# Values of two batches by head on 96 partitions, their keys read in thirds with a stride, three weight loads moved

## The chip, the core and the metric

The kernel runs on one core of a Trainium2 chip, as a single program. Its time is in device microseconds (us). The engines of the core run side by side and wait for one another by semaphores: PE (TensorE: matmuls and transposes into PSUM), DVE (VectorE), ACT (ScalarE), POOL (GpSimd), and SP (SyncE), which here only issues transfers (DMAs). PSUM is the small memory that PE writes, SBUF the working memory of 128 partitions.

## What is computed

Eight batches of attention in two steps, and a layer of eight experts behind it. Everything is fp32.

```python
# q, k, v: 8 batches x 8 heads x 576 x 64; p: 8 x 8 x 32 x 64
p_packed = softmax(p @ k.T / 8) @ v          # 32 packed rows a head
out      = softmax(q @ p_packed.T / 8) @ p_packed
x  = out.transpose(0, 2, 1, 3).reshape(4608, 512)
logits = normed(x) @ normed(expert_emb).T / tau
e  = argmax(logits);  gate = softmax(logits)[e]
y  = gate * (relu(x @ w1[e]) @ w2[e])        # w1: 8 x 512 x 1024, w2: 8 x 1024 x 512
```

## The kernel before

The batches go through the core one after another. The kernel guesses one expert for a whole batch, loads its two weight matrices (w1, 2 MB, and w2, 2 MB), and runs the two matmul layers (`ffn`). While PE does the layers of a batch, the attention of the next one is slipped in between, by generators that are advanced one step at a time. The order on each engine is therefore fixed in the program. For batch 0 it is written out by hand, in the table `PLAN`, whose letters advance `begin` (q), the second softmax of batch 0 (s), the attention of batch 1 (a), the turning of batch 1's queries (d) and the splitting of w2 (w).

`begin` is the attention of batch 0 from an empty chip, and the scores of batch 1. Nothing can hide behind matmuls there; the work is a chain. PE warms up on constants (`WARM`, line 1252). Keys, values and queries of four heads (a group; g is 0 or 1) are loaded (`load_whole`, `load_v`). A loaded key tile, `nat`, has head and i on its 128 partitions, and in a row 18 keys of 64 numbers: key s = 18 i + c. PE turns it in nine blocks of 128 columns (`turn`, line 1264) into PSUM, and ACT or DVE copies the turned blocks into `kT` (tile `spare`). `parity_scores` (line 1296) multiplies the packed rows with the turned keys. It reads 288 of them as nine runs of 32 numbers that stand together. The runs are put in such an order (`blocks`) that the 96 keys of one chunk of weights are those of 32 partitions times three blocks, as `load_v` lays the values out: three transfers for each group, each to 32 partitions, four heads of 1,536 bytes in each partition. `p1_turn` turns the exponentials (line 473), and `pack_values` (line 486) multiplies them with the values.

PSUM tiles of the tag `pf` are three banks in rotation: a tile waits until the copy out of the third tile before it is done. The tile `pu` is one bank of its own, `pt` are two double banks.

Every transfer of SP and ACT waits for the landing of the one eight transfers before it. In the listings of the order this is `waits DMAHW0` to `DMAHW7`, eight semaphores in rotation. The transfers of SP are issued in program order, and one that waits holds up all behind it.

After the scores of batch 0's queries, `begin` issues in one go: the four loads of w2 (`load_w2`, line 960, 512 KB each, two of the eight blocks of w2 in each), the values of batch 1 (`load_v`), and its queries (`load_nat`, line 201, sixteen transfers of 140 KB). Then it turns batch 1's keys and makes its scores. Batch 1's queries are turned on DVE (`flip`, line 298, four of them, into `kt`). In DVE's order they stand between the copies behind PE's matmuls (lines 1072 and 1077) and the rows `ppx` of batch 1 (line 500), which PE then turns (line 510). PE needs all four for the scores of line 277. w2 is split on ACT and POOL (`split_w2`, lines 970 and 971), eight times for a batch, block by block; line 1102 also reads it as it was loaded.

Of the kernel before, what the change touches and what calls it, by code (L numbers as in the profile page):

```python
# [9 lines left out]
F32 = mybir.dt.float32  # L10
# [7 lines left out]
P = 128  # L18
HB = 4
NC5 = 5  # L20
KC = 6
KR = 96
# [5 lines left out]
def kernel(  # L28
# [12 lines left out]
    nc = tc.nc  # L41
# [185 lines left out]
    def load_v(b, g, odd=nc.sync):  # L227
# [36 lines left out]
    def head(g, c):  # L264

        return c ^ g
# [688 lines left out]
    def load_w2(x, e, queue=nc.sync):  # L955
        x.w2r = []
        w2e = w2[e].rearrange("(a p) m -> p a m", p=P)
        for i in range(NF // 2):
# [3 lines left out]
        x.w2s = []  # L962
# [259 lines left out]
    def begin():  # L1222
# [17 lines left out]
        vn = [load_v(0, g, nc.scalar) for g in range(NG)]  # L1240
# [3 lines left out]
        def bank():  # L1244
            return ps.tile([P, 512], F32, name="pf", tag="pf")
# [22 lines left out]
        def blocks(at, to):  # L1268
            return [m % 3 * 3 + m // 3 for m in range(at, to)]

# [19 lines left out]
        def parity_scores(to, w, t, g, at):  # L1290

            t = t[:, g].rearrange("p (c r i) -> p c r i", r=HB, i=32)
            for c in range(HB):
                for par in range(2):
# [4 lines left out]
                        t[hs, :, head(g, c)],  # L1299
# [6 lines left out]
        wx = scaled(pn, nc.vector)  # L1306
# [5 lines left out]
        def one_bank():  # L1312
            return pc.tile([P, 512], F32, name="pu", tag="pu")
# [12 lines left out]
        turn_keys(1, 0, 4, bank(), copies[0])  # L1326
        turn_keys(1, 4, 6, bank(), copies[1])
        pu = one_bank()
        turn_keys(1, 6, 9, pu, copies[0])
        kn1 = [load_whole(k[1], g) for g in range(NG)]  # L1330
        for g in range(NG):
            parity_scores(x.s1[g], wx, kT, g, lambda c: head(g, c))
# [75 lines left out]
        for g in range(NG):  # L1408
            parity_scores(s2[g], x.Tw, qT, g, lambda c: c)
# [21 lines left out]
        for g in range(NG):  # L1431
            turn(kn1[g], pu[:, g * P :], (8,))
        nc.scalar.copy(kT[:, :, 1024:], pu[:, : NG * P].rearrange("p (g s) -> p g s", g=NG))
        for n in range(2 * NG):
            if n:
                yield
            pu = bank()
            turn(kn1[n // 2], pu, blocks(n % 2 * 4, n % 2 * 4 + 4))
            nc.scalar.copy(kT[:, n // 2, n % 2 * 512 : n % 2 * 512 + 512], pu)
        yield  # L1440
        y.halves = True
        for g in range(NG):
            y.s1[g] = turn_bank()
            parity_scores(y.s1[g], wy, kT, g, lambda c: head(g, c))
            yield
# [50 lines left out]
    WARM = (4, 4)  # L1496
# [189 lines left out]
```

## Time and profile before

| | us |
|---|---|
| median of three runs | 412.43 |
| lowest, highest of them | 412.36, 414.54 |
| the profiled execution | 413.43 |
| its span, first to last instruction | 411.8 |
| PE busy | 402.9 |
| DVE, ACT, POOL busy | 310.1, 203.9, 161.2 |

The profiled execution took 413.43 us, of which 411.8 are its span and 1.6 lie around it; it was 1.0 us over the median. The granted TensorE clock is 0.999 of full speed over the span. PE is busy for 98% of the span, so the few microseconds in which it isn't, and those in which it waits inside a row, are what a change outside PE's own work can win.

### The profile page before, as it was taken

How to read it: one execution, taken by the hardware profiler on the slowest of the kernel's cores; microseconds unless marked ns; L12 is line 12 of the kernel's file. 1: busy time of each engine (PE TensorE's matmuls, PEld its weight loads, DVE VectorE, ACT ScalarE, POOL GpSimd, SP SyncE). 2: the span in 40 equal slices, each digit the busy share in tenths (PEclk: the TensorE clock that was granted, in tenths of full speed). 3: DMA queues.
4: the chain of work that ended last, by engine and by line, in shares of the span. 5: the costliest groups of instructions: out<-in, count | busy, mean ns of one | idle time of the engine just before them, and what ended most of it. 6: DMA issues, size and time to landing. Idle time of an engine off the chain costs nothing.

```text
span 411.8 us, 11101 instructions
## 1 busy us (share of the span) xinstructions
PE 402.9 (98%) x4012; PEld 322.4 (78%) x4013; DVE 310.1 (75%) x984; ACT 203.9 (50%) x507; POOL 161.2 (39%) x202
## 2 busy tenths in 40 slices
PE   7999999999999999999999999999999999999995
PEld 3758588697878978698786978789687987879785
DVE  3576888589996889779896899968897698836700
ACT  4677354763257622765138622667237651475201
POOL 2355802337503474047703375035730477030500
PEclk9999999999999999999999999999999999999999
DMA  8999898885889679985897768995799722910022
GB/s 226 337 335 211 217 275 297 223 202 163 249 327 238 163 191 345 286 206 139 215 394 213 206 169 265 332 234 146 203 333 281 200 66 77 391 39 19 8 61 56
DMA packets 42607, 87.93 MB, mean 214 GB/s; under 512 B 11690, under 2 KB 20906, under 8 KB 42546
## 3 DMA queue, kind: packets, MB, share of 16 engines
q1 hardware_dynamic: 35280, 61.44, 54.5%
q0 software_dynamic: 6720, 25.17, 16.7%
q10 hardware_dynamic: 546, 0.54, 0.6%
q8 instruction: 34, 0.56, 0.6%
q14 instruction: 27, 0.22, 0.2%
HBM read 77.68 MB, written 9.44 MB: 212 GB/s over the span
## 4 chain that ended last, share of the span: by engine, by line
PE 90%; DMA 6%; DVE 1%; SPq 0%; ACT 0%; issue 0%; DVEq 0%; ACTq 0%
PE pf L1120 43%; PE pf L1067 23%; PE pf L1102 7%; DMA vn<-in_v 4%; PE pt L995 3%; PE pt L797 3%; PE pt L277 2%; PE pt L403 2%; PE pt L338 2%; PE pu L797 2%; DMA nat<-in_k 1%; DMA nat<-in_q 1%; PE pf L1264 1%; PE pt L1296 0%; PE pu L510 0%; PE pf L486 0%
## 5 line engine op out<-in xcount | busy, mean ns | idle before, releaser
L1120 PE MATMUL pf<-w2s,hT 128*128 128x512 f32 (+1 forms) x792 | 181.5, 387 | 0.0
L1120 PEld LDWEIGHTS pf<-w2s,hT 128*128 128x128 f32 x792 | 143.7, 188 | 38.5 <-issue 10.1
L971 POOL TENSOR_TENSOR w2s<-w2r,w2s 128x512 fp32r<-128x512 f32 x64 | 80.8, 1287 | 73.3 <-ACT w2s L970 68.5
L1067 PE MATMUL pf<-AT,G 128*128 128x288 f32 x720 | 102.3, 299 | 0.3 <-DVE h L1077 0.3
L1067 PEld LDWEIGHTS pf<-AT,G 128*128 128x128 f32 x720 | 97.3, 188 | 4.0 <-issue 1.5
L1072 DVE SCALAR_TENSOR_TENSOR hT<-pf,hT 128x224 fp32r<-128x224 f32 (+1 forms) x128 | 52.3, 413 | 29.0 <-ACT hT L1071 28.6
L1071 ACT ACTIVATE hT<-pf 128x224 fp32r<-128x224 f32 (+1 forms) x128 | 49.3, 386 | 43.0 <-PE pf L1067 40.1
L298 DVE STREAM_TRANSPOSE kt<-nat 128x576 f32<-128x576 f32 x52 | 38.0, 757 | 2.5 <-DMA nat<-in_q 2.3
L1474 ACT ACTIVATE o<-pf,gate 128x512 f32<-128x512 f32 (+1 forms) x41 | 25.9, 634 | 24.4 <-PE pf L1120 16.8
L970 ACT CAST w2s<-w2r 128x512 fp32r<-128x512 f32 x64 | 37.7, 624 | 0.0
L891 POOL MEMSET oh<- 64x8 f32 x8 | 0.8, 98 | 86.2 <-DVE oh L887 86.2
L716 ACT ACTIVATE st<-st 128x576 f32<-128x576 f32 (+1 forms) x17 | 11.1, 658 | 43.8 <-DVE st L713 42.7
L1102 PE MATMUL pf<-w2r,h 128*64 128x256 f32 x256 | 31.5, 385 | 0.0
L1010 DVE TENSOR_TENSOR G<-pt,G 128x1024 fp32r<-128x1024 f32 x14 | 16.5, 1219 | 13.0 <-ACT G L1009 12.9
L933 ACT ACTIVATE lg<-lg 128x40 f32<-128x40 f32 x8 | 1.9, 237 | 48.3 <-DVE lg L929 48.3
L390 POOL TENSOR_TENSOR qs<-p 128x320 f32<-128x320 f32 x12 | 10.5, 877 | 36.9 <-ACT p L371 36.9
L1102 PEld LDWEIGHTS pf<-w2r,h 128*64 128x64 f32 x256 | 16.9, 137 | 8.5 <-PE pu L510 1.0
L810 ACT ACTIVATE scr<-pt 128x512 f32<-128x512 f32 (+1 forms) x32 | 15.7, 491 | 13.8 <-DVE part L851 10.6
L737 ACT CAST AT<-at 128x576 fp32r<-128x576 f32 x15 | 10.1, 675 | 17.9 <-DVE at L731 17.8
L371 ACT ACTIVATE p<-pt,qnm 128x160 f32<-128x160 f32 x48 | 17.8, 398 | 0.0
L960 POOL DMA_DIRECT2D w2r<-in_moe_w x24 | 16.9, 716 | 0.0
L702 DVE STREAM_TRANSPOSE st<-pt 128x288 f32<-128x288 f32 x32 | 13.3, 451 | 0.9 <-PE pt L1296 0.9
(235 smaller groups left out, 518.1 us busy)
## 6 DMA issues: line engine op xcount, KB each, us to landing
nat<-in_q SPq DMA_DIRECT2D x112, 140.0 KB, 3.4
nat<-in_k SPq DMA_DIRECT2D x96, 140.0 KB, 3.5
w1t<-in_moe_w POOLq DMA_DIRECT2D x12, 1024.0 KB, 7.6
w2r<-in_moe_w POOLq DMA_DIRECT2D x24, 512.0 KB, 9.7
out<-o SPq DMA_DIRECT2D x124, 64.0 KB, 2.6
w2r<-in_moe_w SPq DMA_DIRECT2D x8, 512.0 KB, 10.6
vn<-in_v SPq DMA_DIRECT2D x24, 160.0 KB, 3.7
vn<-in_v SPq DMA_DIRECT2D x48, 80.0 KB, 3.7
```

The source lines that it names most:

```text
L298: nc.vector.transpose(kt.rearrange("p (c i) -> p c i", i=32), t)
L371: nc.scalar.activation(x.p1[g][:, n * QW : n * QW + QW], area(x, g)[:, n // 2, n % 2], AF.Exp, bias=x.nm[:, at : at + 1],)
L797: nc.tensor.matmul(to, x.at[at, g, tokens], x.ppx[at, g], start=True, stop=True, tile_position=(64 * half, column),)
L960: queue.dma_start(t, w2e[:, 2 * i : 2 * i + 2, :])
L970: nc.scalar.copy(t[:, 0], raw)
L971: nc.gpsimd.tensor_tensor(out=t[:, 1], in0=raw, in1=t[:, 0].bitcast(F32), op=ALU.subtract)
L1067: nc.tensor.matmul(pf[:, :HS], w, r, start=(n == 0), stop=(n == len(ops) - 1))
L1071: nc.scalar.activation(hT[:, 0, f, cs], pf[:, :n], AF.Relu)
L1072: nc.vector.scalar_tensor_tensor(out=hT[:, 1, f, cs], in0=pf[:, :n], scalar=0.0, in1=hT[:, 0, f, cs].bitcast(F32), op0=ALU.max, op1=ALU.su ...
L1102: nc.tensor.matmul(pf[64 * hf : 64 * hf + 64, :256], h4[:, f], x.w2r[f // 2][:, f % 2, hf * 256 : hf * 256 + 256], start=(f == 0), stop=(f ...
L1120: nc.tensor.matmul(pf[:, :w], hT[:, a, f, c * P : (c + 1) * P], x.w2s[f][:, m, at : at + w], start=(f == 0 and i == 0), stop=(f == NF - 1 ...
L1474: nc.scalar.activation(o[:, :w], pf[:, :w], AF.Copy, scale=x.gate[:, c : c + 1])
```

## The change

There are four edits.

- `load_v` brings the values of a head in one transfer to 96 partitions: partition p holds keys 6 p to 6 p + 5, 1,536 bytes for each head. A group takes four transfers instead of three. All eight of batch 0 are SP's; before, two of its six were ACT's. Batches 2 to 7 load by `load_runs` and are as they were.
- A chunk of 96 keys is now every sixth key, so the scores must come out in that order. The nine blocks of a group are turned in thirds, as they lie, three to a bank (`turn_keys`), for batch 0 and batch 1 alike. `key_scores` reads the turned keys with the third as the innermost index: consecutive numbers of the moving operand stand 384 numbers (1,536 bytes) apart. The output is as wide as before. The scores of the queries (line 1296 with `tw`) read as before.
- The packed rows of batch 0 are turned ahead of the keys on PE, and the second of the two warm-up matmuls is 384 columns wide instead of 512.
- Three of the four loads of batch 0's w2 stand behind batch 1's values and queries on SP.

```diff
     def load_v(b, g):
         t = sb.tile([P, KC * HB * D], F32, name="vn", tag="vn", bufs=2)
         t = t.rearrange("p (h w) -> p h w", h=HB)
-        s = v[b, g * HB : (g + 1) * HB].rearrange("h (i c) d -> i h (c d)", c=NCB)
-        for a in (0, 2, 1):
-            (odd if a == 2 else nc.sync).dma_start(
-                t[32 * a : 32 * a + 32], s[:, :, a * KC * D : (a + 1) * KC * D]
-            )
+        s = v[b, g * HB : (g + 1) * HB].rearrange("h (p c) d -> h p (c d)", c=KC)
+        for h in range(HB):
+            nc.sync.dma_start(t[:KR, h], s[h])
...
-        def turn_keys(g, at, to, pu, copy):
-            pu = pu[:, : (to - at) * P]
-            turn(kn[g], pu, blocks(at, to))
-            copy(kT[:, g, at * P : to * P], pu)
+        def turn_keys(nat, g, a, pu, copy):
+            turn(nat, pu, range(3 * a, 3 * a + 3))
+            copy(kT[:, g, 3 * a * P : 3 * a * P + 3 * P], pu[:, : 3 * P])
+
+        def key_scores(x, w, g):
+            t = kT[:, g].rearrange("p (a c r i) -> p r c i a", a=3, c=3, r=HB)
+            parity_scores(x.s1[g], w, t, lambda c: head(g, c), g)
+
+        wx = packed_turn(scaled(pn, nc.vector), one_bank())
...
-        turn_keys(0, 0, 4, bank(), copies[0])
-        turn_keys(0, 4, 8, bank(), copies[1])
-        turn_keys(0, 8, 9, x.s1[0][:, 384:512], copies[1])
-        wx = packed_turn(wx, one_bank())
-        turn_keys(1, 0, 4, bank(), copies[0])
-        turn_keys(1, 4, 6, bank(), copies[1])
+        for n in range(5):
+            turn_keys(kn[n // 3], n // 3, n % 3, bank(), copies[n != 1 and n != 3])
         pu = one_bank()
-        turn_keys(1, 6, 9, pu, copies[0])
+        turn_keys(kn[1], 1, 2, pu, copies[0])
...
-        load_w2(x, x.e)
+        load_w2(x, x.e, pairs=range(1))
         for g in range(NG):
             loaded[1, 2 * NPR + g] = load_v(1, g)
         prefetch(order[1, NPR] + 3)
+        load_w2(x, x.e, pairs=range(1, NF // 2))
         yield
         wy = packed_turn(wy, bank())
-        pu = bank()
-        for g in range(NG):
-            turn(kn1[g], pu[:, g * P :], (8,))
-        nc.scalar.copy(kT[:, :, 1024:], pu[:, : NG * P].rearrange("p (g s) -> p g s", g=NG))
-        for n in range(2 * NG):
-            if n:
+        for n in range(3 * NG):
+            turn_keys(kn1[n // 3], n // 3, n % 3, bank(), nc.scalar.copy)
+            if n not in (0, 3):
                 yield
-            pu = bank()
-            turn(kn1[n // 2], pu, blocks(n % 2 * 4, n % 2 * 4 + 4))
-            nc.scalar.copy(kT[:, n // 2, n % 2 * 512 : n % 2 * 512 + 512], pu)
-        yield
...
-    WARM = (4, 4)
+    WARM = (4, 3)
```

SP's order from batch 0's second weights on. `w2r` are the four loads of w2, `vn` the values of batch 1, `nat<-in_q` its queries, `nat<-in_k` the keys of batch 2. Before:

```order
L960 DMA w2r<-in_moe_w 128x2x512
L960 ISA
L960 DMA w2r<-in_moe_w 128x2x512
L960 ISA
L960 DMA w2r<-in_moe_w 128x2x512
L960 ISA
L960 DMA w2r<-in_moe_w 128x2x512
L232 DMA vn<-in_v 32x4x384 x6
L201 DMA nat<-in_q 32x1120 x16
L201 DMA nat<-in_k 32x1120 x4
```

and changed:

```order
L959 DMA w2r<-in_moe_w 128x2x512
L232 DMA vn<-in_v 96x384 x8
L201 DMA nat<-in_q 32x1120 x16
L959 ISA
L959 DMA w2r<-in_moe_w 128x2x512
L959 ISA
L959 DMA w2r<-in_moe_w 128x2x512
L959 ISA
L959 DMA w2r<-in_moe_w 128x2x512
L201 DMA nat<-in_k 32x1120 x4
```

Twenty-four transfers instead of six and three weights stand between the first and the second load of w2.

ACT's order where batch 1's keys are turned. `wp` are the packed rows, `spare` the turned keys, `st` the exponentials of batch 0's second softmax (two, each behind POOL's subtraction), `g` rows of the first layer. Before:

```order
L1284 COPY wp<-pf 128x2x128
L1433 COPY spare<-pf 128x2x128
L1439 COPY spare<-pf 128x512
L716 ACTIVATE st<-st 128x288 x2
L1439 COPY spare<-pf 128x512 x3
L1047 COPY g_550<-pf 128x512 x2
```

and changed:

```order
L1279 COPY wp<-pf 128x2x128
L1305 COPY spare<-pf 128x384 x2
L714 ACTIVATE st<-st 128x288 x2
L1305 COPY spare<-pf 128x384 x4
L1045 COPY g_557<-pf 128x512 x2
```

Four copies instead of three stand behind the exponentials; with the three banks of `pf`, the matmul that fills `g` first waited for the first of these three, and waits for the second of these four.

## Rows read from the trace of the kernel before

**Rows 1.** The page: busy time, share of the span and instructions of each engine.

```profile
PE 402.9 (98%) x4012; PEld 322.4 (78%) x4013; DVE 310.1 (75%) x984; ACT 203.9 (50%) x507; POOL 161.2 (39%) x202
```

**Rows 2.** Chain of waits, 0 to 60 us: start, duration, what held the end.

```profile
1.46 5.33 DMA nat<-in_k
...
21.27 14.76 DMA vn<-in_v
...
36.85 4.73 DMA nat<-in_q
```

**Rows 3.** Timeline of PE at the start: start, duration, instruction, idle time before it.

```profile
1.23 3.78 PE L1252 MATMUL pf<-fill 128*128 128x512 f32 x4 [1.23 <-DVE mask L72]
5.21 1.06 PE L1264 MATMUL pf<-ident,nat 128*128 128x128 f32 x8 [0.20 <-DMA nat<-in_k]
...
17.22 0.72 PE L1296 MATMUL pt<-spare,tw 64*32 64x288 f32 x16
...
22.13 0.63 PE L1035 MATMUL pf<-w1t,tw 64*32 64x512 f32 x4 [0.54 <-ACT spare L1439]
```

**Rows 4.** Timeline of ACT at the start.

```profile
20.77 0.82 ACT L716 ACTIVATE st<-st 128x288 f32<-128x288 f32 x2
21.50 1.54 ACT L1439 COPY spare<-pf 128x512 f32<-128x512 f32 x3
```

**Rows 5.** Timeline of DVE, 39 to 49 us.

```profile
41.66 0.78 DVE L298 STREAM_TRANSPOSE kt<-nat 128x576 f32<-128x576 f32 x1 [1.58 <-DMA nat<-in_q]
...
44.95 0.59 DVE L500 SCALAR_TENSOR_TENSOR ppx<-pt,ri,mask 128x128 f32<-128x128 f32 x2
...
48.02 0.78 DVE L298 STREAM_TRANSPOSE kt<-nat 128x576 f32<-128x576 f32 x1 [0.68 <-DMA nat<-in_q]
```

**Rows 6.** Timeline of PE, 24 to 60 us.

```profile
28.57 5.12 PE L1067 MATMUL pf<-at,g 128*128 128x288 f32 x20
...
43.66 1.08 PE L1102 MATMUL pf<-w2r,h 128*64 128x256 f32 x8
45.34 0.59 PE L510 MATMUL pu<-ident,ppx 128*128 128x128 f32 x2 [0.59 <-DVE ppx L500]
...
48.27 1.75 PE L277 MATMUL pt<-kt,T 64*32 64x288 f32 x32
```

**Rows 7.** Chain of waits over the whole span, at lines 277 and 510.

```profile
48.34 1.68 PE pt L277 x32
...
96.50 0.22 PE pu L510 x2
...
100.55 1.13 PE pt L277 x32
```

**Rows 8.** Timeline of SP's transfers, 16 to 52 us.

```profile
18.86 2.32 SPq L960 DMA_DIRECT2D w2r<-in_moe_w  x4
...
32.85 11.19 SPq L201 DMA_DIRECT2D nat<-in_q  x16
```

**Rows 9.** Tile w2r, 16 to 55 us: issue to landing of its four loads.

```profile
DMA to landing us min/median/max: 9.6/11.6/14.5
```

**Rows 10.** Windows: length, engines' busy time, clock, DMA share, GB/s; weights, values, queries.

```profile
24.00:29.00 5.00, 4.99 (x41) 2.79 (x31) 2.97 (x9) 3.21 (x7) 1.88 (x3) 1.00 1.05 398
30.00:35.00 5.00, 5.00 (x28) 4.18 (x26) 3.90 (x9) 4.13 (x10) 4.12 (x4) 1.00 1.10 193
38.00:45.00 7.00, 6.75 (x136) 5.75 (x134) 5.23 (x21) 5.99 (x15) 3.29 (x3) 1.00 0.94 251
```

**Rows 11.** Timeline of ACT, 41 to 43.5 us.

```profile
41.78 0.62 ACT L970 CAST w2s<-w2r 128x512 fp32r<-128x512 f32 x1
42.29 0.36 ACT L1071 ACTIVATE hT<-pf 128x224 fp32r<-128x224 f32 x1
```

**Rows 12.** Lines 1447 and 707 alone: durations in ns, times, forms.

```profile
L1447 DVE TENSOR_REDUCE fold<-ident x1: 380/380/380, 34.9 to 34.9; 128x32 f32<-128x128 f32 x1
L707 DVE TENSOR_REDUCE mx<-st x17: 453/752/754, 19.0 to 349.4; 128x18 f32<-128x576 f32 x15, 128x9 f32<-128x288 f32 x2
```

More of the change, by code (lines that the diff above doesn't have):

```diff
@@ L953, in load_w1, with load_w2 @@
         x.w1t = w1t
-    def load_w2(x, e, queue=nc.sync):
-        x.w2r = []
+    def load_w2(x, e, queue=nc.sync, pairs=range(NF // 2)):
+        if 0 in pairs:
+            x.w2r, x.w2s = [], []
         w2e = w2[e].rearrange("(a p) m -> p a m", p=P)
-        for i in range(NF // 2):
+        for i in pairs:
             t = sb.tile([P, 2, DM], F32, name="w2r", tag="w2r", bufs=NF // 2)
@@ L961, in load_w2 @@
             x.w2r.append(t)
-        x.w2s = []
     def split_w2(x):
@@ L1239, in begin @@
         next(emb_gen)
-        vn = [load_v(0, g, nc.scalar) for g in range(NG)]
+        vn = [load_v(0, g) for g in range(NG)]
         qn = [load_whole(q[0], g) for g in range(NG)]
@@ L1266, in turn @@
                 )
-        def blocks(at, to):
-            return [m % 3 * 3 + m // 3 for m in range(at, to)]
         def scaled(t, eng):
@@ L1288, in packed_turn, with parity_scores @@
             return to
-        def parity_scores(to, w, t, g, at):
-            t = t[:, g].rearrange("p (c r i) -> p c r i", r=HB, i=32)
+        def parity_scores(to, w, t, at, g):
             for c in range(HB):
@@ L1298, in parity_scores @@
                         w[hs, g * P + 32 * at(c) : g * P + 32 * at(c) + 32],
-                        t[hs, :, head(g, c)],
+                        t[hs, head(g, c)],
                         start=True,
@@ L1305, in begin, with one_bank @@
         x.halves = True
-        wx = scaled(pn, nc.vector)
+        def one_bank():
+            return pc.tile([P, 512], F32, name="pu", tag="pu")
+        def turn_keys(nat, g, a, pu, copy):
[5 more added lines that the diff above has]
+        wx = packed_turn(scaled(pn, nc.vector), one_bank())
         next(emb_gen)
@@ L1310, in begin @@
         copies = (nc.scalar.copy, nc.vector.tensor_copy)
[L1312 to L1318 removed]
         for g in range(NG):
             x.s1[g] = turn_bank()
[L1322 to L1327 removed]
+        for n in range(5):
+            turn_keys(kn[n // 3], n // 3, n % 3, bank(), copies[n != 1 and n != 3])
         pu = one_bank()
[L1329 removed]
+        turn_keys(kn[1], 1, 2, pu, copies[0])
+        key_scores(x, wx, 0)
         kn1 = [load_whole(k[1], g) for g in range(NG)]
[L1331 to L1332 removed]
+        key_scores(x, wx, 1)
         nc.tensor.matmul(pu[:, 384:385], fill[:1], tau1, start=True, stop=True)
@@ L1408, in begin @@
         for g in range(NG):
-            parity_scores(s2[g], x.Tw, qT, g, lambda c: c)
+            t = qT[:, g].rearrange("p (c r i) -> p r c i", r=HB, i=32)
+            parity_scores(s2[g], x.Tw, t, lambda c: c, g)
         pts = [one_bank(), bank()]
@@ L1427, in begin @@
         prefetch(order[1, NPR] + 3)
+        load_w2(x, x.e, pairs=range(1, NF // 2))
         yield
         wy = packed_turn(wy, bank())
-        pu = bank()
-        for g in range(NG):
-            turn(kn1[g], pu[:, g * P :], (8,))
-        nc.scalar.copy(kT[:, :, 1024:], pu[:, : NG * P].rearrange("p (g s) -> p g s", g=NG))
-        for n in range(2 * NG):
-            if n:
+        for n in range(3 * NG):
+            turn_keys(kn1[n // 3], n // 3, n % 3, bank(), nc.scalar.copy)
+            if n not in (0, 3):
                 yield
-            pu = bank()
-            turn(kn1[n // 2], pu, blocks(n % 2 * 4, n % 2 * 4 + 4))
-            nc.scalar.copy(kT[:, n // 2, n % 2 * 512 : n % 2 * 512 + 512], pu)
-        yield
         y.halves = True
@@ L1443, in begin @@
             y.s1[g] = turn_bank()
-            parity_scores(y.s1[g], wy, kT, g, lambda c: head(g, c))
+            key_scores(y, wy, g)
             yield
```

2 lines of the change are left out of this document (1 added, 1 removed).

## The prediction

> **What bounds the kernel now.** I read four views, in this order. The page first: PE is busy for 402.9 of 411.8 us [rows 1], so outside PE some 9 us are to be had at most, and where PE doesn't wait nothing is. Then the chain of waits for the first 60 us: it begins on the landing of batch 0's keys (issued at 1.46, 5.33 us), runs over PE, DVE and ACT without slack, and at 21.27 it leaves PE for a transfer of batch 1's values that lands 14.76 us later; from there it goes to a transfer of batch 1's queries [rows 2]. Behind 54 us the chain is PE alone, in a pattern that repeats from batch to batch. So the change can only act before 54 us, and what it wins or loses there is carried to the end unaltered. Third, the timelines of PE, ACT and DVE in that stretch, for the idle time in front of each instruction: PE waits 0.54 us for a copy of turned keys [rows 3] and 0.59 us for `ppx` [rows 6], and DVE twice waits for queries, 1.58 and 0.68 us [rows 5]. Last, SP's transfers, for what stands in front of those queries: four loads of w2 from 18.86 on, then values, and the first query is issued at 32.85 only [rows 8].
>
> **The start, up to 19 us: 0.** The warm-up takes 3.78 us for two matmuls (four records) [rows 3]. [...] 128 of 1,024 columns less are 0.47 us less; the two transposes of packed rows take that place. Both lie in front of the keys, for which PE waited 0.20 us [rows 3], and that wait is the cover: if it went, the difference of the two, about 0.1 us, would show. Batch 0's values now come in eight transfers of SP alone. The last of them waits for the landing of the second keys, at 6.8 us [rows 2]; at the slowest rate of the trace, 193 GB/s [rows 10], 1.18 MB take 6.1 us, so they are there before 13 us even then, and `pack_values` is where they are wanted, from 12 us on. The keys may land earlier, since ACT's two loads of values no longer share the queues with them: two of 0.2 MB at 398 GB/s [rows 10] are 1.0 us at the very most, if both went ahead of the keys. The keys stand in SP's queue in front of all values, though, so I take 0 and keep -0.4 as the far end.
>
> **Turning batch 1's keys: +0.3.** PE's 18 transposes stay 18, but they fill six banks instead of five, out of three. The first matmul on w1 (line 1035) came at 22.13, after 0.54 us of waiting for the first of three copies of 512 behind the two exponentials [rows 3, 4]. It now needs the second of four copies of 384. Three copies of 512 took 1.54 us [rows 4], 0.51 each; three quarters of that are 0.39, as an estimate, with some fixed part 0.42. First copy before: ends at 21.50 + 0.59. Second copy now: 21.50 + 0.42 + 0.48, that is 0.3 us later. PE runs from there to the first layer without a gap, so all of it is on the path. Ends: 0.1, if ACT starts sooner because its first two copies are shorter, and 0.5.
>
> **Batch 1's queries earlier: -1.5.** In front of them now stand w1, one load of w2 and the values; three loads, 1.57 MB, are gone, which at 398 GB/s [rows 10] are 3.9 us. The first load of w2 lands at 18.86 + 9.6 = 28.5 at the earliest of its row [rows 8, 9]. Values, 1.18 MB, take 3.0 us at 398 or 6.1 at 193 GB/s, and the first quarter of the queries, four transfers of 0.143 MB, 2.3 us at 251 GB/s [rows 10]. That is 33.8 to 36.9 us, and DVE asked for it at 41.66 - 1.58 = 40.08 [rows 5]; the last quarter comes 6.8 us later, at 43.7 at the latest, and is wanted at 46. So both waits of DVE go, also if the values are no faster on 96 partitions than on 32. What is next: without its 1.58 us DVE would have `ppx` at 43.4 instead of 44.95 [rows 5]. PE ends the four matmuls in front of line 510 at 44.74 [rows 6], so PE itself is then last, and its 0.59 us of idle time goes. The two transposes of line 510 took 0.59 us there and 0.22 in the next batch [rows 6, 7], since the second waits for the second `ppx`: another 0.37. Line 277 took 1.68 us and in the next batch 1.13 [rows 7], because the last query is turned while it runs: 0.55. Sum 1.51, all on PE's path. Ends: 0.6, if only the idle time goes, and 1.8.
>
> **The three weights behind the queries: 0.** They are issued when the ninth to eleventh of the queries' transfers have landed and follow the sixteenth. The first is cast at 41.78, and behind this cast ACT holds the `hT` of line 1071 at 42.29 [rows 11], DVE waits for that `hT`, and `ppx` and all of the last paragraph stand behind it in DVE's order. Some slack is there: DVE comes to it at about 43.2. Behind the second and third cast ACT holds only casts, and POOL, which splits at its own pace, is not done before 50 us. So one landing counts. Queries end at 28.5 + 3.0 + 9.1 = 40.6 (398 and 251 GB/s) to 43.7, and 0.52 MB more are 1.3 us: 41.9 to 45.0, against 42.4 at which it begins to hurt. As the first load lay 9.6 us in the queue behind traffic that is now partly gone (batch 1's keys will have landed before w1 is issued), I take the early end and 0, with +2.6 at the other end. This is the thinnest place of the sum.
>
> **Reading the keys with a stride: 0.** This is the cost that the trace doesn't show: no matmul in it reads its moving operand in single steps. Sixteen records of line 1296 take 0.72 us [rows 3]; one record of 288 columns by itself takes 5.12 / 20 = 0.256 us [rows 6], so eight of them run side by side, in two passes of some 0.27. There are eight such passes with the new order, two for each group and batch, and PE is waited for behind all of them. A gain is excluded, since the pass is already as long as one record alone. From above, the nearest row is DVE's: line 1447 reads 128 numbers that stand 32 apart and takes 0.380 us, while line 707 takes 0.453 for 288 and 0.752 for 576 in a row [rows 12], which is 1.04 ns a number and 0.29 us for 128. The stride costs 0.09 us / 128 = 0.73 ns a number there. If PE paid that for each column, a pass would be 0.21 longer, and eight +1.7. The farthest end: if the four streams that read the same partitions side by side had to take turns, a pass would be four times as long, 1.0 us, and eight +5.9. I take 0, because a matmul record of fp32 spends 0.256 / 288 = 0.89 ns on a column, about the time DVE needs for a number in a row, and a single extra access may hide in it; the number is uncertain and decides the range.
>
> [...]
>
> **The sum.** 0 + 0.3 - 1.5 + 0 + 0 = -1.2 us. The profiled execution's 411.8 of span would be 410.6, with the 1.6 around it 412.2 us; it lay 1.0 over the median, so the median goes from 412.43 to 411.2. Half a percent, which is about what a measurement of this kernel can tell from no change, is 2.06 us: below 410.4 is faster, above 414.5 slower. The sum is too small to show.
>
> **The rivals.**
> - *The start wins as well.* The keys land 0.4 us earlier and the bank in front of line 1035 costs 0.1 instead of 0.3, and line 277 gains its 1.8: 412.43 - 0.4 + 0.1 - 1.8 = 410.3. For it speaks that the chain starts on that landing; against it that SP's keys are first in the queue in both kernels.
> - *The strided read costs what DVE's row says.* -1.2 + 1.7: 412.9. [...]
> - *The strided read costs a pass each of its four streams* (slower). Place: line 1290 in the new code, in batch 0's chain at 8 us and in batch 1's scores at 22. Price +5.9, less some 0.6 that the second group of batch 0 hides behind DVE's maximum: 412.43 - 1.2 + 5.3 = 416.5. It decides from 0.4 us more a pass on, that is when a pass takes 0.67 instead of 0.27. For it: four streams do read the same 64 partitions. Against it: nothing in the trace shows PE held by its operands.
> - *The first moved weight is late.* It lands at 44 to 45, 2 us after the cast is due: `ppx` comes when it came before, or 1 us later; only line 277's 0.55 stays won: 412.2 to 413.7.
> - *The queries are late still*, the change doing nothing for them: 412.43 + 0.3 = 412.7. Against it stand 3 us or more of slack in each bound above.
>
> **How the numbers follow.** My sum 0.47, a start that wins 0.10, DVE's price 0.17, four streams in turn 0.12, a late weight 0.12, late queries 0.02. The likeliest gives 411.2 us. The range leaves out the four streams and a little below the sum: 410.1 to 414.0, the low end being the first rival less a run's scatter of some 0.2, the high end the late weight and the scatter. Faster by over 0.5%: the first rival and a small part of my sum, 0.13. Slower: the four streams and the worst of the late weight, 0.15. The rest, 0.72, is within 0.5%.
>
> **What would show it.** DVE's two waits for queries gone and no idle time at line 510; line 277 down to about 1.1 us; line 1033 at about 22.4 with 0.8 us of waiting in front; a record of line 1290 as long as before, and sixteen in 0.7 us. I am wrong if sixteen of them take 1.1 or more, if ACT idles in front of its third cast of w2 near 42 us, or if the first keys' landing moves by more than 0.4.

## The result: slower by half a percent, and where it shows

The changed kernel takes 414.96 us (median of 13 runs, 414.48 to 417.14), against 412.47 (13 runs, 412.29 to 417.83) for the kernel before beside it: a ratio of 1.0051 with a 95% interval of [1.0031, 1.0072]. That is slower by about half a percent, 2.1 us by the ratio. The prediction was 411.2 with a range of 410.1 to 414.0, so the time lies outside the range and on the other side of no change.

The profiled execution of the changed kernel took 415.29 us, of which 413.7 are its span; that is 1.9 more span than before. The page of the changed kernel, busy time and then the two queues of the kind `instruction`:

```profile
PE 403.3 (97%) x4012; PEld 323.2 (78%) x4013; DVE 310.1 (75%) x984; ACT 203.9 (49%) x508; POOL 161.6 (39%) x202
...
q8 instruction: 34, 0.56, 0.6%
q14 instruction: 29, 0.24, 0.2%
```

Beside [rows 1], PE is 0.4 us busier and ACT has one busy instruction more, 508 instead of 507. The kernel before has 27 packets of q14, this one 29. The one instruction, and one of the two packets, small as they are, turn out to go with the loss.

To find the place, I followed one instruction after the other on PE in both traces. First five rows of before (start, duration, instruction, and in brackets the idle time before it with what ended it): the turning of batch 0's second keys (those of its second group of heads), batch 0's scores, `pack_values`, the turn of batch 1's packed rows, and the first layer.

```profile
6.92 0.84 PE L1264 MATMUL pf<-ident,nat 128*128 128x128 f32 x6 [0.32 <-DMA nat<-in_k]
...
8.03 1.36 PE L1296 MATMUL pt<-spare,wp 64*32 64x288 f32 x32
...
12.04 1.67 PE L486 MATMUL pf<-vn,p1T 96*32 96x64 f32 x96
...
19.06 0.44 PE L1282 MATMUL pf<-ident,wp 128*128 128x128 f32 x2
...
24.32 3.18 PE L1067 MATMUL pf<-at,g 128*128 128x288 f32 x12
```

The same places on PE in the changed kernel, and with them its answers to [rows 3] and [rows 6]:

```profile
7.49 0.85 PE L1262 MATMUL pf<-ident,nat 128*128 128x128 f32 x6 [0.27 <-DMA nat<-in_k]
...
8.60 1.54 PE L1290 MATMUL pt<-spare,wp 64*32 64x288 f32 x32
...
19.46 0.44 PE L1277 MATMUL pf<-ident,wp 128*128 128x128 f32 x2
...
22.65 0.55 PE L1262 MATMUL pf<-ident,nat 128*128 128x128 f32 x3 [0.92 <-ACT spare L1305]
23.13 0.63 PE L1033 MATMUL pf<-w1t,tw 64*32 64x512 f32 x4
...
25.66 0.51 PE L1065 MATMUL pf<-at,g 128*128 128x288 f32 x1
...
44.55 1.08 PE L1100 MATMUL pf<-w2r,h 128*64 128x256 f32 x8
45.56 0.44 PE L508 MATMUL pu<-ident,ppx 128*128 128x128 f32 x2
...
48.35 1.20 PE L275 MATMUL pt<-kt,T 64*32 64x288 f32 x32
```

The lag of the changed kernel is +0.57 at the second keys and at batch 0's scores, +0.40 at the packed rows of batch 1 (some was absorbed in a wait for the queries' copies), +1.00 at the first row on w1 (22.13 before), and +1.34 at the first layer. Then it falls: +0.89 at 43.66, +0.22 at line 508, which no longer waits. At the last activation of the kernel it is -0.26. ACT's last activation in each trace, before and then changed:

```profile
407.45 0.47 ACT L1474 ACTIVATE o<-pf,gate 128x256 f32<-128x256 f32 x1 [2.40 <-DMA out<-o]
```

```profile
407.19 0.47 ACT L1462 ACTIVATE o<-pf,gate 128x256 f32<-128x256 f32 x1 [2.40 <-DMA out<-o]
```

So in this pair of executions the changed kernel is ahead by 0.26 us when the computing ends. From the end of that activation to the end of the span it then takes 6.0 us instead of 3.9: 2.1 us, more than the 1.9 that this pair differs by, lie behind the last arithmetic, in a place that the prediction had not looked at. The profiled execution of before lay 1.0 us over its median, that of the changed kernel 0.3. Against the medians, which differ by 2.5 us (2.1 by the ratio), those 2.1 are all of the loss or all but 0.4 of it.

What stands there is a branch. At its end the kernel tests whether any row was guessed to the wrong expert, and jumps over a fallback block, which is not executed for these inputs. All engines jump. The instructions of that line in the trace, for each engine's sequencer (count, duration in ns, first and last start in us), for DVE and ACT, before:

```profile
L1596 DVEq EVENT_SEMAPHORE  x2: 21/21/21, 394.4 to 394.5; - x2
...
L1596 ACTq EVENT_SEMAPHORE  x2: 17/17/17, 409.9 to 410.0; - x2
...
L1596 DVEq COMPARE_BRANCH  x1: 72/72/72, 391.4 to 391.4; - x1
...
L1596 ACTq COMPARE_BRANCH  x1: 54/54/54, 409.5 to 409.5; - x1
```

and changed:

```profile
L1584 DVEq EVENT_SEMAPHORE  x2: 21/21/21, 394.0 to 394.1; - x2
...
L1584 ACTq EVENT_SEMAPHORE  x2: 17/17/17, 412.0 to 412.0; - x2
...
L1584 DVEq COMPARE_BRANCH  x1: 72/72/72, 391.1 to 391.1; - x1
...
L1584 ACTq COMPARE_BRANCH  x1: 54/54/54, 409.1 to 409.1; - x1
```

From ACT's branch to its next instruction it took 0.4 to 0.5 us before and 2.8 to 2.9 in the changed kernel. DVE's branch has that long form (2.9 to 3.0 us) in both, but at 391 us, where nobody waits for DVE. SP closes the program, and it waits for ACT. SP's own waits from 400 us on, changed kernel (in total, times, longest):

```profile
SPq L1670 <- ACTq L1584: 1.4, 1, 1.4
```

Before, that row doesn't exist. The difference is 2.4 us a branch, and q14 has 4 packets from 407 us on in the changed kernel where it has 3 before. That ACT waits there for the code behind its jump was my guess, theory A in the expectations below; no trace shows what it waits for.

### The profile page after: what moved, and what is told of

It reads as the page before. It is cut to its first block, busy times and chain, and to the rows that moved or that the text cites. A ratio compares the mean times of both kernels' runs of the same rounds, so it can differ in the third digit from the quotient of the medians.

```text
span 413.7 us, 11105 instructions
## 1 busy us (share of the span) xinstructions
PE 403.3 (97%) x4012; PEld 323.2 (78%) x4013; DVE 310.1 (75%) x984; ACT 203.9 (49%) x508; POOL 161.6 (39%) x202
## 4 chain that ended last, share of the span: by engine, by line
PE 93%; DMA 2%; ACT 2%; DVE 1%; issue 0%; SPq 0%; POOL 0%; DVEq 0%; ACTq 0%
PE pf L1118 43%; PE pf L1065 24%; PE pf L1100 7%; PE pt L993 3%; PE pt L795 3%; PE pt L401 2%; PE pt L275 2%; PE pt L336 2%; PE pu L795 2%; DMA nat<-in_k 1%; PE pf L1262 1%; PE pt L1290 1%; PE pt L471 1%; PE pu L508 0%; ACT p L456 0%
```

## Experiments

Each kernel was timed beside the kernel before on the same chip. The ratios are to that, and the medians of kernels on different chips compare only roughly. a_hint, b_act1, b_far and b_w2 ran on one chip; h_w2old, h_w23, b_w23 and h_flat on a second; a_again, a_w2old, h_rot and h_rot_flat on a third; c_mix and c_mixa on a fourth; c_back and a_back on a fifth. "End" below is the stretch from the end of the last activation to the end of the span in the profiled execution.

### The branch at the end

**a_hint**: the changed kernel; the mark at the last stores that announces the branch (a hint, for SP alone in both kernels) names ACT as well.

```diff
-                tc.mark_branch_hint_location("rest", engines=[mybir.EngineType.SP])
+                tc.mark_branch_hint_location(
+                    "rest", engines=[mybir.EngineType.SP, mybir.EngineType.Activation]
+                )
```

> [...] Theory A (code fetch): the changed kernel ends later because ACT's jump over the block that isn't executed lands on code that has to be fetched first, 2.8 us from the branch to the next instruction against 0.46 before; with the mark ACT goes on within 0.6 us, the span shrinks by 1.9 to 2.3 us, and the time is 412.2 to 412.9, that of the kernel before. Theory B (stores): ACT waits there for the landing of its own last two stores; then the mark does nothing and the time stays at 414.5 to 415.5.

Measured: 414.51 us, ratio 1.0044 [1.0025, 1.0063]. The branch is mended, and the end falls from 6.0 to 4.7 us, not to the 3.9 of before:

```profile
L1586 ACTq EVENT_SEMAPHORE  x2: 17/17/17, 410.2 to 410.3; - x2
...
L1586 ACTq COMPARE_BRANCH  x1: 68/68/68, 409.8 to 409.8; - x1
```

The expectation failed: the time falls by 0.3 to 0.6 us by the ratios (beside the changed kernel and its repetition a_again), within the intervals, and not by 2. The profiled execution lost elsewhere, at the second weights (below).

**b_act1**: the kernel before, with one more ACT instruction at the start, which repeats an activation of a single number.

```diff
         nc.scalar.activation(seen, ones[:1], AF.Exp)
+        nc.scalar.activation(seen, ones[:1], AF.Exp)
```

> The kernel before with one instruction more on ACT: the 1 x 1 exponential that loads ACT's table at the start is issued twice, 0.2 us at 3.7 us, where ACT is idle for 1.3 us. ACT then has 610 instructions ahead of the branch, as in the changed kernel, instead of 609. Theory A (code fetch, set by the place of the code): ACT's jump takes 2.8 us instead of 0.46 and the kernel 414.5 to 415. Theory B (stores) or any other cause that lies in the change's own work: 412.3 to 412.7, as before.

Measured: 414.48 us, ratio 1.0045 [1.0028, 1.0062]; the end takes 5.8 us. None of the four edits is in this kernel, and it loses nearly what the change loses:

```profile
L1597 ACTq EVENT_SEMAPHORE  x2: 17/17/17, 411.1 to 411.1; - x2
...
L1597 ACTq COMPARE_BRANCH  x1: 54/54/54, 408.1 to 408.1; - x1
```

```profile
SPq L1683 <- ACTq L1597: 1.9, 1, 1.9
```

**b_far**: the kernel before, with one more ACT instruction inside the fallback block. It is never executed; it only moves the branch's target one instruction further off.

```diff
                     nc.vector.memset(a, 0.0)
+                nc.scalar.copy(ge[:, :, 0], ge[:, :, 0])
```

> The kernel before with one ACT copy more in the block that is skipped: nothing that is executed differs, only the jump's target lies one instruction further. Theory A, with the target's place deciding: 414.5 to 415, ACT's jump 2.8 us. Theory A, with the branch's own place deciding: 412.3 to 412.7. Theory B: 412.3 to 412.7.

Measured: 412.98 us, ratio 0.9998 [0.9974, 1.0023]; the branch takes 0.46 us and the end 3.9, as before:

```profile
L1596 ACTq EVENT_SEMAPHORE  x2: 17/17/17, 408.3 to 408.4; - x2
...
L1596 ACTq COMPARE_BRANCH  x1: 54/54/54, 407.9 to 407.9; - x1
```

So what counts is where the branch itself stands in ACT's stream, one instruction further on, and not how far it jumps. The changed kernel has one more ACT instruction in front of it, waits and issues of transfers counted: 610 instead of 609 in the built program. The other profiles bear that out. Without the hint, ACT's branch took 0.46 us in all four kernels with 609 instructions (before, b_far, b_w2, b_w23) and 2.8 to 3.0 in all five with 610 (changed, a_again, a_w2old, a_back, b_act1); with it, 0.48 in all nine. Nor is it chance from one execution to the next: the lowest of 12 executions of a_again was 414.67 us, 1.9 over the median of before beside it. Why just this place decides was not settled.

### The three moved loads of w2

**b_w2**: the kernel before with this edit alone (`load_w2` with `pairs`, three loads behind the queries).

```diff
-        load_w2(x, x.e)
+        load_w2(x, x.e, pairs=range(1))
...
         prefetch(order[1, NPR] + 3)
+        load_w2(x, x.e, pairs=range(1, NF // 2))
```

> The kernel before with the loads of batch 0's second weights in the changed order and nothing else; values, keys and warm-up are as before, and ACT has as many instructions as before. If the term of 1.5 us for the earlier queries is right and comes from the order of the loads alone: DVE doesn't wait for queries, line 510 has no idle time ahead of it, and the time is 410.8 to 411.4. If the earlier queries also need values on 96 partitions (the values, on 32, landing later): half of it, 411.5 to 412. If the late weights take it back: 412.2 to 413.7.

Measured: 414.86 us, ratio 1.0060 [1.0034, 1.0085]. The edit that was to win 1.5 us loses 2.5 by itself, by the ratio. ACT's third cast and, behind it, PE at line 510 and line 1102:

```profile
45.63 0.62 ACT L970 CAST w2s<-w2r 128x512 fp32r<-128x512 f32 x1 [3.62 <-DMA w2r<-in_moe_w]
```

```profile
47.38 0.68 PE L510 MATMUL pu<-ident,ppx 128*128 128x128 f32 x2 [2.50 <-DVE ppx L500]
47.99 1.98 PE L1102 MATMUL pf<-w2r,h 128*64 128x256 f32 x8
```

That is the rival of the late first weight, by its mechanism: the cast waits, ACT holds back an `hT`, DVE waits for that, `ppx` is late and PE idles. In this execution a second price followed: behind PE's idle 2.50 us the granted clock was 0.50 from 48 to 51 us, and eight matmuls of line 1102 took 1.98 us, where they take 1.08 at 1.00. It was 1.6 us over the median of b_w2, so not every execution pays that. In a_hint the same cast waited 2.23 and PE 1.28 us. In the profiled execution of the changed kernel it waited 0.68, and PE did not idle.

**h_w2old** is a_hint with the four loads in one piece again; **h_w23** is a_hint with only the last two loads moved; **b_w23** is the kernel before with only those two moved. Against a_hint, first h_w2old, then h_w23:

```diff
-        load_w2(x, x.e, pairs=range(1))
+        load_w2(x, x.e)
...
-        load_w2(x, x.e, pairs=range(1, NF // 2))
```

```diff
-        load_w2(x, x.e, pairs=range(1))
+        load_w2(x, x.e, pairs=range(2))
...
-        load_w2(x, x.e, pairs=range(1, NF // 2))
+        load_w2(x, x.e, pairs=range(2, NF // 2))
```

> The changed kernel with ACT's jump mended (the mark of the run a_hint, 414.51) and batch 0's four loads of second weights back in one piece ahead of batch 1's values; values by head and keys in thirds stay. Theory A: moving the weights costs more than earlier queries win, since the third cast on ACT waits for its weights (2.2 us in the trace of a_hint, with 1.28 us of idle time on PE ahead of line 508). Then this kernel doesn't wait there, and takes 413.2 to 413.8. Rival: the queries are late again, as in the profiled execution of the kernel before (1.5 us on PE's path): 414.6 to 415.5.

> The same base, with two of the four loads of second weights moved instead of three: pair 1, whose first cast is the third on ACT, stays ahead of the values. Theory A: the wait at the third cast goes, the queries are still 1 us or more ahead of need: 413.0 to 413.5, and at most as much as with all four loads in one piece. Rival: no loading order makes a difference of more than 0.4 us, and what a_hint is over the kernel before comes from its keys and values: 414.2 to 414.8.

> The kernel before with two of the four loads of second weights (pairs 2 and 3) behind batch 1's queries, all else as before. Theory A: in most executions of the kernel before the queries come nearly in time (a wait of 0.25 us in the trace of b_far, whose executed part is the same), so there is little to win: 412.0 to 412.5, fewer executions above 413. Rival: the profiled execution of before, with 1.5 us lost to late queries, is the usual one: 411.0 to 411.5.

Measured: h_w2old 413.02, ratio 1.0003 [0.9992, 1.0015]; h_w23 413.61, 1.0016 [1.0003, 1.0028]; b_w23 413.44, 1.0021 [1.0004, 1.0039]. Moving two instead of three costs less, but it is no gain on either side: in b_w23 the casts still wait, 0.33 and 1.18 us, while PE doesn't idle at line 510, and 0.9 us by the ratio are lost that its profile doesn't show. That execution was the shortest of its twelve, 0.9 us under the median, so what the others lose stays open.

h_w2old also shows what became of the queries. In it they stand behind all four loads of w2, as in the kernel before, and DVE nevertheless has all of them in time:

```profile
40.23 0.77 DVE L296 STREAM_TRANSPOSE kt<-nat 128x576 f32<-128x576 f32 x1
...
42.57 0.77 DVE L296 STREAM_TRANSPOSE kt<-nat 128x576 f32<-128x576 f32 x1
...
45.55 0.77 DVE L296 STREAM_TRANSPOSE kt<-nat 128x576 f32<-128x576 f32 x1
...
46.59 0.78 DVE L296 STREAM_TRANSPOSE kt<-nat 128x576 f32<-128x576 f32 x1
```

Even b_far, which executes exactly what the kernel before executes, waits for one of them only (its profiled execution lay 1.2 us under its median):

```profile
46.58 0.78 DVE L298 STREAM_TRANSPOSE kt<-nat 128x576 f32<-128x576 f32 x1 [0.25 <-DMA nat<-in_q]
```

b_act1, whose loads stand as before too, has no such wait (0.5 us under its median). So of three profiled executions with that order, the waits of 1.58 and 0.68 us in [rows 5] are in one alone.

**a_again** is the changed kernel, unaltered, and **a_w2old** the changed kernel with w2 in one piece and the branch left as it is.

> The changed kernel once more, unaltered, beside the next three on one chip: 414.5 to 415.3, ACT's jump again 2.8 us. If the jump's length were chance and not set by the program, some executions would lie near 412.7.

> The changed kernel with the four loads of second weights back in one piece and nothing else undone; the jump isn't mended. Theory A (moved weights cost, the jump costs 2 us by itself): 0.5 to 1.5 us under the changed kernel run beside it, 413.5 to 414.4, with a narrow scatter, no wait at ACT's third cast and ACT's jump still 2.8 us. Rival (the moved loads are what wins in the change): 0.3 to 1.5 us above it.

Measured: a_again 415.30, ratio 1.0058 [1.0036, 1.0079]; a_w2old 414.87, 1.0050 [1.0029, 1.0070]. With the branch unmended, putting the loads back wins 0.4 us, within the intervals. From a_w2old to h_w2old only the hint is added, and that wins 1.85 us (1.9 by the ratios, as the two ran on different chips). So with the loads in one piece the branch is, by the ratio, all that the changed kernel loses by. With them moved there are two losses, and they don't add up: the late weight costs from nothing to 0.4 us while the branch is long, but 1.5 between a_hint and h_w2old, and 2.5 in b_w2. The chip alone doesn't decide that: in h_flat (below), on another chip than a_hint, the third cast waited 1.39 and PE 0.43 us. The last of the four loads was issued at 40.1 us in the changed kernel and at 40.0 in a_hint, yet the third cast began at 43.61 and at 44.61. What makes the weight land so differently, and why it cost nothing in both profiles of the changed kernel, stays open.

### The strided read

**h_flat**: a_hint, with the stride moved from PE's read to the copies' write, so that `key_scores` reads runs again.

```diff
-            copy(kT[:, g, 3 * a * P : 3 * a * P + 3 * P], pu[:, : 3 * P])
+            copy(kT[:, g].rearrange("p (x a) -> p a x", a=3)[:, a], pu[:, : 3 * P])
...
-            t = kT[:, g].rearrange("p (a c r i) -> p r c i a", a=3, c=3, r=HB)
+            t = kT[:, g].rearrange("p (c r w) -> p r c w", c=3, r=HB)
```

**h_rot_flat** is h_rot (below) with the same edit.

> The base a_hint (414.51) with the stride moved from PE's read to the copies: each copy out of a bank writes its 384 columns 3 numbers apart, so that the keys stand in the order of the scores and line 1290 reads 96 numbers in a row. Theory A: the stride costs PE 0.067 us a pass (0.333 between passes in the trace of the changed kernel, 0.266 before); with eight passes on the path this kernel takes 0.5 us less, 413.9 to 414.1, and the passes are 0.267 apart. Rival: the copies pay for the stride instead, 0.48 to 0.56 us or more each, and the time stays within 0.2 of 414.5. If the stride were not read by PE at a price at all, the passes stay 0.333 apart.

> h_rot with the stride in the copies, as in h_flat, now without the scatter of the late weights. Theory A (PE's stride costs 0.5 us on the path and is worth more than the copies' stride): 0.2 to 0.5 us under h_rot. Rival: the copies, 0.69 instead of 0.48 us on ACT and 0.68 instead of 0.56 on DVE in the trace of h_flat, lie on the same path with six of them in batch 0's chain and two more ahead of line 1033: equal to h_rot within 0.2, or up to 0.5 above it.

Measured: h_flat 413.79, ratio 1.0033 [1.0017, 1.0049], against 1.0044 for a_hint; h_rot_flat 413.38, 1.0011 [0.9989, 1.0033], against 1.0004 for h_rot. The matmuls and the copies between 0 and 26 us (busy us, mean ns of one), in the changed kernel:

```profile
L1290 PE MATMUL pt<-spare,wp 64*32 64x288 f32 x64 | 4.1, 496 | 0.0
L1305 ACT COPY spare<-pf 128x384 f32<-128x384 f32 x8 | 3.5, 479 | 1.5 <-PE pf L1262 1.5
```

in the kernel before:

```profile
L1296 PE MATMUL pt<-spare,wp 64*32 64x288 f32 x64 | 3.4, 411 | 0.0
```

and in h_rot_flat:

```profile
L1306 ACT COPY spare<-pf 128x384 f32<-128x384 f32 x8 | 5.0, 705 | 0.8 <-PE pf L1263 0.8
L1291 PE MATMUL pt<-spare,wp 64*32 64x288 f32 x64 | 3.5, 411 | 0.1
```

A record of 288 columns read with the stride takes 496 ns instead of 411, the same 64 records 0.7 us more in sum (4.1 less 3.4). The flat read gives that back, and each of ACT's copies pays 0.23 us (705 less 479) for it; there are twelve such copies, on ACT and DVE, in the same chain. The stride's price moved from one engine to others, and the ratios show nothing won.

### The values' transfers, the end and the start

**h_rot**: h_w2old with the values of the first two heads of a group in one transfer, so three transfers a group as before. **c_mix**: h_w2old with the values of batch 1 in two transfers a group. **c_mixa**: c_mix with head 1 of each group of batch 0's values on ACT's queue.

```diff
-        for h in range(HB):
+        nc.sync.dma_start(t[:KR, :2], s[:2].rearrange("h p w -> p h w"))
+        for h in (2, 3):
             nc.sync.dma_start(t[:KR, h], s[h])
```

and for c_mix, with the line that c_mixa adds to it:

```diff
-        for h in range(HB):
-            nc.sync.dma_start(t[:KR, h], s[h])
+        n = 1 if b == 0 else 2
+        for h in range(0, HB, n):
+            queue = nc.scalar if b == 0 and h == 1 else nc.sync      # c_mixa
+            queue.dma_start(t[:KR, h : h + n], s[h : h + n].rearrange("h p w -> p h w"))
```

> The run h_w2old (413.02) with the values of two heads in one transfer, three transfers a group instead of four: as many as before, so that the last four stores sit on the same four of the eight semaphores as in the kernel before (the fifth to the eighth of the list that SP walks through at the end, not the first to the fourth). Theory A (SP's list): what lies behind the last activation shrinks from 4.74 to 3.9 to 4.4 us and the time is 412.2 to 412.7. Rival (the length of the tail comes from the stores themselves): it stays 4.7 and the time 413.0.

> The run h_w2old (values by head, keys in thirds, weights in one piece, ACT's jump mended; 413.02) with batch 1's values in two transfers a group instead of four, so that the kernel has as many transfers as before and the last stores sit on the last four semaphores of SP's list; batch 0's values stay in eight transfers of SP. If the tail shrinks as in h_rot (4.74 to 4.01) and the scatter of h_rot came from batch 0's transfers of two heads: 412.2 to 412.5, no lower than the kernel before by more than 0.4. Rival: the start's scatter is that of values by head in any form: 412.6 to 413.4.

> c_mix with two of batch 0's eight transfers of values (head 1 of each group) on ACT's queue. If the queue decides: the second keys land at 6.8 to 7.1 us, as in all traces without values by head, and the time is 0.2 to 0.6 under c_mix with less scatter. If the shape of the transfers decides: the second keys land anywhere from 6.5 to 8.4 and the time is that of c_mix within 0.3.

Measured: h_rot 413.15, ratio 1.0004 [0.9984, 1.0024]; c_mix 412.84, 1.0010 [0.9997, 1.0023]; c_mixa 413.01, 1.0014 [1.0001, 1.0027]. c_mixa's time is that of c_mix within 0.2, so nothing speaks for the queue of batch 0's values. What h_rot and c_mix were for shows at the end, which takes 4.7 us in h_w2old, 4.0 in h_rot and c_mix, and 3.9 in c_mixa. SP passes nine semaphores, the eight in rotation among them, one by one before it closes the program, and with four more transfers in the kernel the last stores have others of the eight. SP's waits from 400 us on, h_w2old and then c_mix:

```profile
SPq L1585 <- SPq L1585: 1.2, 3, 0.5
SPq L1671 <- PEq L1671: 0.7, 2, 0.5
```

```profile
SPq L1586 <- SPq L1586: 0.7, 2, 0.5
SPq L1672 <- PEq L1672: 0.4, 2, 0.2
```

So 0.7 us of the end go with the number of transfers: with the hint, four kernels with four more than before end in 4.7 us (a_hint, h_w2old, h_w23, h_flat), and five with as many as before in 3.9 to 4.3. That it is the place of the last stores among the eight is argued from SP's waits, not tested by itself. The times don't show it: the medians of h_w2old and h_rot differ by 0.1.

**c_back** is c_mix, and **a_back** the changed kernel, each with the packed rows of batch 0 turned behind the first three thirds of the keys again, and a warm-up of eight blocks.

```diff
-        wx = packed_turn(scaled(pn, nc.vector), one_bank())
+        wx = scaled(pn, nc.vector)
...
         for n in range(5):
+            if n == 3:
+                wx = packed_turn(wx, one_bank())
...
-    WARM = (4, 3)
+    WARM = (4, 4)
```

> The mended kernel (branch hint on ScalarE, second weights in one piece, batch 1's values in two transfers a group) with one thing more put back: the packed rows of batch 0 are turned behind the first three thirds of the keys, as in the kernel before, and the warm-up has eight blocks again. Theory A, the order at the start costs: TensorE no longer waits for the packed rows ahead of the keys, no transposes at the lower clock behind that wait, first scores of batch 0 at 8.0 to 8.4 us, 412.0 to 412.6, ratio 0.998 to 1.000. Theory B, the keys' landing alone sets the start: first scores still at 8.0 to 10 us with the second key landing, 412.8 to 413.2, ratio about 1.001.

> The changed kernel with only that order put back (packed rows behind the first three thirds, warm-up of eight blocks). ScalarE's instructions stay 610, so its branch at the end stays at 2.8 to 3.0 us. Theory A: 0.2 to 0.8 below the changed kernel, 414.2 to 414.8, ratio 1.003 to 1.005. Theory B: as the changed kernel, 414.9 to 415.3, ratio 1.005 to 1.006.

Measured: c_back 412.74, ratio 0.9992 [0.9979, 1.0006]; a_back 415.21, 1.0054 [1.0040, 1.0069]. The first fits theory A, the second theory B. Their intervals overlap those of c_mix and of the changed kernel, so a price of the order is not shown. The profile of c_back fits neither story whole:

```profile
5.85 2.15 PE L1263 MATMUL pf<-ident,nat 128*128 128x128 f32 x9 [0.84 <-DMA nat<-in_k]
...
10.28 1.56 PE L1291 MATMUL pt<-spare,wp 64*32 64x288 f32 x32
```

There the first keys came late although nothing of the change stood in front of them, nine transposes took 2.15 us where [rows 3] has eight in 1.06, and the scores came 2.2 us later than before. That execution was the longest of its twelve, 1.9 us over the median. In c_mixa, PE waited for the packed rows ahead of the keys, and 15 transposes took 3.47 us:

```profile
5.23 0.66 PE L1279 MATMUL pu<-ident,wp 128*128 128x128 f32 x2 [0.64 <-DVE wp L1270]
5.68 3.47 PE L1264 MATMUL pf<-ident,nat 128*128 128x128 f32 x15
```

So the start depends on three things that differ from execution to execution: when the keys land, when the packed rows land, and how long PE's transposes start 0.213 us apart, instead of 0.109. The third is the clock: the trace's record of the granted clock has its first entry, 1.00, at 5.10 us in the kernel before, 6.98 in the changed one, 10.10 in c_mixa and 10.39 in c_back, where three transposes still took 0.85 us at 8.95 and at 9.51 (0.49 at 7.61 in the kernel before). In the changed kernel a transpose ahead of that entry is 421 ns long and 0.213 us from the next one, behind it 272 and 0.109. There is no entry for the time ahead; that the clock was about 0.50 there is an estimate, from the spacing twice as long and from the eight matmuls of b_w2 (1.98 us at 0.50, 1.08 at 1.00). PE had idled 0.84 us ahead of its keys in c_back, and 0.64 ahead of the packed rows in c_mixa; why the clock rose so late there wasn't tested. Of the second keys the profiles show more: in the five kernels with the start of before, PE had them by 7.2 us; with eight transfers of batch 0's values on SP, PE waited for them until 7.4 to 8.6 in six kernels of ten. How much of this, and of the packed rows' landing, the change's order adds is not settled. No kernel of these beats the kernel before by what can be measured.

## Why the prediction was wrong

- **"What it wins or loses there is carried to the end unaltered."** This is the step that failed, with "the change can only act before 54 us" in front of it. It was taken from a chain of waits that ends with the last activation and says nothing of what comes behind it. One more instruction on ACT made the branch at the end 2.4 us longer, and the end took 6.0 us instead of 3.9. b_act1 makes the long branch without the change and loses 1.9; a_hint takes 1.3 of the 2.1 off the end, and the other 0.7 or 0.8 go with the four additional transfers (4.7 to 4.0 in h_rot and c_mix). In time, a_w2old and h_w2old price the branch at 1.85; a_hint, with the weights moved, wins only 0.3 to 0.6. None of the rivals had it; the 0.15 for slower stood on other mechanisms.
- **Queries earlier, -1.5.** The signs that were named came: DVE's two waits are gone, line 508 doesn't idle and line 275 takes 1.20 us. But the gain is one against the profiled execution, which lay 1.0 us over the median. The prediction took that 1.0 off to get at the median, and took off the waits as well, though they were part of what had held that execution up. In b_far those waits are nearly absent without any change; its span is 410.2 where the profiled one of before is 411.8, and its time, 411.83, is 0.6 under the median of before. So against the median the term was worth 0 to 0.6 and not 1.5, and no run shows that it was won.
- **The three weights, 0 with +2.6 as the end.** The end was right and the value was not: the price is 0 to 0.4 in the changed kernel, 1.5 beside a_hint and 2.5 in b_w2. The landing was reckoned as 41.9 to 45.0, and the early end was taken for a reason of the queue alone. In the changed kernel the cast got its weight at 43.61, inside these bounds; in b_w2 at 45.63, past the late one. The prediction called it the thinnest place, and its own sign of being wrong, ACT idle in front of the third cast, came (0.68 us), though at no cost to PE in that execution.
- **Stride, 0.** A record is longer by 85 ns, so a pass by 0.07 to 0.08, eight by some 0.6. At batch 0 the lag grows by 0.18 up to `pack_values`, and more than that is absorbed by 19 us; batch 1's, 0.34 from the first row on w1 to the first layer, is on the path. Per number that is 0.23 to 0.29 ns, a third of DVE's row of 0.73. The four streams do not take turns (+5.9 would have been that). So the assumption that the access hides in the column's 0.89 ns was wrong in kind and small in size.
- **Turning, +0.3.** Right in size: from `pack_values` to the first row on w1 it took 10.09 us before and 9.98 in b_far (12.15 to 22.13), and 10.34 in the changed kernel (10.35 in h_w2old), so +0.25 to +0.36; counted from batch 1's packed rows alone it is 0.3 (h_w2old) to 0.6 (changed). The copy was the wrong one, here and where ACT's order is listed: PE waits 0.92 us for the first copy behind the exponentials, since the last three transposes need its bank, and then still has these three to do.
- **Start, 0.** +0.57 in the profiled pair, and all of it is the second keys: PE took them up at 6.92 us before and at 7.49 in the changed kernel, after waiting for their transfer in both. The prediction weighed only that keys land earlier. Its sum held the difference of columns against the keys' wait, and also missed that the packed rows are a transfer of their own, which PE now needs ahead of the keys. And it is a single number for something that lies anywhere between -0.2 and +2.2 in the profiles here.

Together, against the medians: what lies before the last activation comes to 0 by the ratio or +0.4 by the medians, where the sum had -1.2 and, without its 1.5, +0.3; the end comes to +2.1.

## What to carry to other kernels

Look at what comes behind the last arithmetic, on each engine, before you say that a gain is carried to the end: a jump or a closing wait there can cost more than the change is worth, and one instruction added far ahead of it can turn it on. Where an engine takes a branch on the path, try the hint that SP has here: on ACT it took 2.4 us off the branch. In the time that showed with the weights in one piece (h_w2old) and hardly with them moved (a_hint). And when a profiled execution lies over the median, its waits may be that excess; look at a second one before you count them as something to be won.

## What the runs showed of the hardware

- A taken branch took 0.46 to 0.48 us or 2.8 to 3.0 us on ACT, in kernels that differ by one instruction ahead of it or by the hint. The long form came with 4 packets of q14 from 407 us on (changed kernel, b_act1), the short one with 3 (before, b_far, a_hint); one instruction more behind the branch changed nothing.
- A matmul of fp32 with a moving operand read at a stride of 1,536 bytes cost 20% more a record (496 against 411 ns); an ACT copy that writes at a stride of three numbers cost 47% more (705 against 479).
- Behind the same warm-up of eight blocks, the first entry of the granted clock came at 5.10 us in the kernel before and at 10.39 in c_back, and the transposes stood 0.109 us apart in the one and 0.213 for most in the other.
- Behind 2.50 us of idle PE in b_w2 the granted clock was 0.50 from 48 to 51 us, and eight matmuls took 1.98 us instead of 1.08.
- Four transfers more in a program went with an end that was 0.7 us longer; that the cause is which of the eight semaphores the last stores use is argued.
